# A convolution loop's store moved to another DMA queue, its filter stores made later, and its drain put in another order

## The chip, the cores and the metric

The kernel runs on one core of one Trainium2 chip. That core has TensorE (PE, matrix products[...]), VectorE (DVE), ScalarE (ACT), GpSimd (POOL) and SyncE (SP, which here only starts transfers), and 16 DMA engines. Each engine works through its own instructions in their order; a transfer is started by an instruction of SP, ACT or POOL and runs beside them. The metric is device time of one execution in microseconds, the median of several runs; lower is better.

## The reference

Two blocks in a row, all in float32, batch B = 4, length S = 12544, width D = 128:

```python
h_filt = (np.maximum(pos_emb @ w1, 0) @ w2) * window      # S x D, window = exp(-0.01 * position)
u = x * v
Uf = np.fft.rfft(u, n=2 * S, axis=1)
Hf = np.fft.rfft(h_filt, n=2 * S, axis=0)
y = np.fft.irfft(Uf * Hf, n=2 * S, axis=1)[:, :S]
t = (x * y).reshape(B * S, D)
out = np.maximum(np.maximum(t @ m1, t @ m2), t @ m3) @ m_out   # m1..m3 128 x 768, m_out 768 x 128
```

A long convolution of every channel with one filter, by way of the frequency domain, a gate, and then a feed-forward block with a maximum of three products.

## The kernel before, in words

The transforms are matrix products with tables. A sequence is split in 128 points by 98 blocks; a *first* stage turns each block column into N1 = 90 frequencies (`u_first`, result in `spec`), a *second* stage finishes the forward transform for a pair of frequencies g, the spectrum is multiplied with the filter's, a *third* stage goes back, and its result z is stored in DRAM (`zd`). A last stage, later, reads `zd` (`t_load`), finishes the inverse transform and goes on into the feed-forward block.

The order of all work is written out by hand: every engine gets its instructions in the order in which Python emits them. A prologue (0 to about 117 us) prepares the filter's first stage, the feed-forward weights and the first stage of batch 0. Then comes **the first loop** (lines 992 to 1025, about 117 to 303 us), which the change is about. It runs over s = 0 to 47, with NK = 45 pairs, and is software-pipelined. Iteration s does:

- `s_second(s)` (L943, PSUM `gps`): the filter's second stage on PE, for which POOL has written `minus` (`s_minus`, L931), the negative of a part of its input, one buffer; ACT copies the result to `G` (L948)
- `g_second(s)` (L156, PSUM `ps` in pool `cps`): the data's second stage; ACT copies half of it to `eo` (L187)
- `g_swap(s-1)` on ACT (L547, L548), which makes `xs`
- `s_filter(s-1)` (L961, PSUM `sps`, one buffer of two banks): the filter's spectrum; ACT copies it to `ht` (L966, two buffers), and POOL starts two stores of it to `hd` in DRAM (L969), for the other batches
- `g_third(s-3)` (L156): third stage; ACT copies it to `zs` (L577, two buffers) and ACT itself starts the store to `zd` (L578)
- `g_re`, `g_im`, `g_unfold` of s-2 and `g_butterfly(s)` on DVE (L553, L557, L558, L565, L181, L182): product with the filter (`ht`), unfolding to `ab` for the third stage, and the next input `xt`
- SP starts the loads of the two weight tables, `wf` three iterations ahead for the second stages, and `wi` for the third (L843)

In some of the last iterations there is also work for batch 1: loads (`u_load`), the product x times v on DVE (`u_mul`, L365), and two `u_turn`s at a time, each four transposes on PE (L370) and a copy on ACT (L377).

**The drain** follows: from s = NK on, third stages of the last pairs, six *folds* (`fold`: a transpose of a weight block on PE, L923, a copy `w1t` on ACT, L925, and a product accumulated in `pl`), which give the matrix `lin`, two more turns, and twelve half *units* (`unit`: `u_first` of half a group, PE L417, ACT `high` L426, DVE `spec` L428), the first stage of batch 1. Before, folds and units are strewn between the third stages by the table `drain`.

[...] here three of pool `cps` (tag cv), two of `gps`, two for `sps` and one for `pl`. Before, second and third stages, turns, folds and units all share the three of `cps`.

After the drain, DVE forms `even` from the first loaded `zt` (L678, L679), PE makes the first last-stage products, and the main loop starts with products into `hps` (323.94 us before). From there on PE is busy nearly without a break.

Of the kernel before, what the change touches and what calls it, by code (L numbers as in the profile page):

```python
# [10 lines left out]
FP32 = mybir.dt.float32  # L11
# [5 lines left out]
P = 128  # L17
# [74 lines left out]
def kernel(  # L92
# [15 lines left out]
    nc = tc.nc  # L108
    NG, _, _, B, NB = x.shape
    FO, S = posT.shape  # L110
    D = w2.shape[1]
    DFF = moe_w1.shape[1]
    NF = DFF // P
    NK = N1 // 2
# [7 lines left out]
    hd = dram.tile([NK, P, 512], FP32, name="hd")  # L122
# [29 lines left out]
    def halves_mm(out, lhsT, rhs, start, stop):  # L152


        for h in range(2):
            nc.tensor.matmul(out[64 * h:64 * h + 64], lhsT[:, 64 * h:64 * h + 64], rhs,  # L156
                             start=start, stop=stop, skip_group_check=True)
# [188 lines left out]
    us, uts, ws, hts, eos, xts, xss, abs_, pss, sqs, zss = ({} for _ in range(11))  # L346
# [20 lines left out]
    def turn(u, ps):  # L367
        a, _ = us.pop(u)
        for i in range(4):
            nc.tensor.transpose(ps[0:NB, i * P:(i + 1) * P], a[:, i, :], eye[:])  # L370

    def u_turn(u):
        if u % 2 == 0:
            uts[u] = uts[u + 1] = utp.tile([NB, 16, 2, 32], FP32, tag="uT", name="uT")
        ps = state["turn"].tile([P, 512], FP32, tag="cv", name="pst")
        turn(u, ps)
        nc.scalar.copy(uts[u][:, 8 * (u % 2):8 * (u % 2) + 8],  # L377
                       ps[0:NB, :].rearrange("n (s t r) -> n s r t", s=8, r=2))
# [153 lines left out]
    def g_second(g):  # L532
        ps = state["cv"][1].tile([P, 512], FP32, tag="cv", name="ps2")
        second(ps, ws.pop((g, 0)), g)
        eo = state["cv"][0].tile([P, 2, D], FP32, tag="eo", name="eo", bufs=2)
        evens(ps, eo)
        pss[g], eos[g] = ps, eo

    def g_butterfly(g):
        xt = state["cv"][0].tile([P, 2, 2, D], FP32, tag="x", name="xt", bufs=state["xb"])  # L540
        butterfly(pss.pop(g), eos.pop(g), xt)
        xts[g] = xt
# [8 lines left out]
    def g_re(g):  # L551
        xt = xts[g]
        nc.vector.tensor_tensor(out=xt[:], in0=xt[:], in1=hts[g][:, 0], op=ALU.mult)  # L553

    def g_im(g, apart=False):
        xt, xs = xts[g], xss.pop(g)
        nc.vector.tensor_tensor(out=xs[:], in0=xs[:], in1=hts.pop(g)[:, 1], op=ALU.mult)  # L557
        (nc.gpsimd if apart else nc.vector).tensor_tensor(  # L558
            out=xt[:], in0=xt[:], in1=xs[:], op=ALU.add)

    def g_unfold(g):
        y = xts.pop(g)
        ab = state["cv"][0].tile([P, 2, 2, D], FP32, tag="ab", name="ab", bufs=2)
        for q, op in enumerate((ALU.add, ALU.subtract)):
            nc.vector.tensor_tensor(out=ab[:, :, q, :], in0=y[:, :, 0, :], in1=y[:, :, 1, :],  # L565
                                    op=op)
        abs_[g] = ab

    def g_third(g):
        w, ab = ws.pop((g, 1)), abs_.pop(g)  # L570
        ps = state["cv"][1].tile([P, 512], FP32, tag="cv", name="ps3")
        for k in range(2):
            for q in range(2):
                halves_mm(ps[:, (2 * k + q) * D:(2 * k + q + 1) * D], w[:, k, q, :],
                          ab[:, k, q, :], k == 0 and q == 0, True)
        zs = state["cv"][0].tile([P, 2, 256], FP32, tag="z", name="zs", bufs=2)
        nc.scalar.copy(zs[:].rearrange("p k f -> p (k f)"), ps[:])  # L577
        nc.scalar.dma_start(  # L578
            zd[0][2 * g:2 * g + 2].rearrange("k c t f -> (c t) k f"), zs[:])

    def conv_steps(b, done):
# [259 lines left out]
    def load_dir(g, a):  # L841
        w = lwp.tile([P, 2, 2, P], FP32, tag=f"w{a}", name="wt")
        nc.sync.dma_start(w[:].rearrange("p k r m -> p (k r m)"), wt_d[g, :, a, :])  # L843
        return w
# [31 lines left out]
    for f in range(0, FO, 4):  # L876
        quad([hs[:, f + i] for i in range(4)], (f1h[:, 0], f1h[:, 1]), specH[:, :, :, f:f + 4])
        u, k = divmod(f // 4, 4)
# [27 lines left out]
    for i in (1, 2):  # L906
# [5 lines left out]
    cvp = pro.enter_context(tc.tile_pool(name="cvp0", bufs=3))  # L912
    cps = pro.enter_context(tc.tile_pool(name="cps0", bufs=3, space=PSUM))
    gps = pro.enter_context(tc.tile_pool(name="gps", bufs=2, space=PSUM))
    sps = pro.enter_context(tc.tile_pool(name="sps", bufs=1, space=PSUM))
    state = {"cv": (cvp, cps), "turn": cps, "xb": 2,
             "bank": lambda: cps.tile([P, 512], FP32, tag="cv", name="ps1")}
    pl = sps.tile([D, 512], FP32, name="pl")
    Gs, minus = {}, {}

    def fold(f):
        pt = cps.tile([P, 512], FP32, tag="cv", name="pt")
        nc.tensor.transpose(pt[:, 0:D], w_sb[0][:, f * P:(f + 1) * P], eye[:])  # L923
        w1t = cvp.tile([P, 2, D], FP32, tag="eo", name="w1t", bufs=2)
        nc.scalar.copy(w1t[:, 0], pt[:, 0:D])  # L925
        return lambda: halves_mm(pl[:, 0:D], w1t[:, 0], wo_sb[:, f, :], f == 0, f == NF - 1)

    def s_minus(g):

        m = cvp.tile([P, 2, FO], FP32, tag="minus", name="minus", bufs=1)  # L930
        nc.gpsimd.tensor_single_scalar(m[:], specH[:, 2 * g:2 * g + 2, 0], -1.0, op=ALU.mult)  # L931
        minus[g] = m
# [18 lines left out]
    def s_filter(g):  # L951


        G = Gs.pop(g)
        ps = sps.tile([P, 1024], FP32, tag="h", name="sps")
        for ri in range(2):
            for k in range(2):
                for q in range(2):
                    for h in range(2):
                        at = 512 * q + (2 * ri + k) * D  # L960
                        nc.tensor.matmul(  # L961
                            ps[64 * h:64 * h + 64, at:at + D],
                            G[64 * q:64 * q + 64, k, ri, :], w2x[64 * q:64 * q + 64],
                            start=(ri == 0 and k == 0), stop=True, skip_group_check=True)
        ht = cvp.tile([P, 2, 2, 2, D], FP32, tag="ht", name="ht", bufs=2)
        nc.scalar.copy(ht[:].rearrange("p r k q d -> p (r k) q d"),  # L966
                       ps[:].rearrange("p (q m d) -> p m q d", q=2, d=D))
        for c in range(2):
            nc.gpsimd.dma_start(hd[g, 64 * c:64 * c + 64],  # L969
                                ht[64 * c:64 * c + 64, c].rearrange("p k q d -> p (k q d)"))  # L970
        hts[g] = ht

    EARLY = 6
    loads = dict(zip((NK - 16, NK - 14, NK - 12, NK - 9, NK - 8, NK - 4), range(EARLY)))
    muls = dict(zip((NK - 13, NK - 11, NK - 10, NK - 5, NK - 3, NK - 1), range(EARLY)))
    turns = {NK - 9: 0, NK - 4: 2}
    folded = []

    def folding(f):
        folded.append(fold(f))  # L980
        if len(folded) > 1:
            folded.pop(0)()

    def unit(u):
        for h in range(2):
            u_first(u, 2 * h, 2)

    drain = {NK: [lambda: folding(0), lambda: folding(1), lambda: folded.pop()()],
             NK + 1: [lambda: folding(2), lambda: folding(3), lambda: folded.pop()(),
                      lambda: unit(0), lambda: unit(1)]}  # L990
    s_minus(0)
    for s in range(NK + 3):
        if s < NK:
            ws[s, 0] = wf[s]
            s_second(s)
            if s + 1 < NK:
                s_minus(s + 1)
            g_second(s)
            wf.pop(s)
            if s + 3 < NK:  # L1000
                wf[s + 3] = load_dir(s + 3, 0)
        if 1 <= s <= NK:
            g_swap(s - 1)
            s_filter(s - 1)
        if s >= 3:
            ws[s - 3, 1] = wi.pop(s - 3)
            g_third(s - 3)
            if s < NK:
                wi[s] = load_dir(s, 1)
        if 2 <= s <= NK + 1:  # L1010
            g_re(s - 2)
            g_im(s - 2)
            g_unfold(s - 2)
        if s < NK:
            g_butterfly(s)

        if s in muls:
            u_mul(muls[s])
        if s in turns:
            u_turn(turns[s])  # L1020
            u_turn(turns[s] + 1)
        if s in loads:
            u_load(1, loads[s])
        for job in drain.get(s, ()):
            job()
    u_turn(4)
    u_turn(5)
    folding(4)
    folding(5)
    folded.pop()()  # L1030
    nc.scalar.copy(lin[:], pl[:, 0:D])
    for u in range(2, 6):
        unit(u)
    pro.close()


# [11 lines left out]
    cvp = conv.enter_context(tc.tile_pool(name="cvp", bufs=3))  # L1048
    hps = ctx.enter_context(tc.tile_pool(name="hps", bufs=1, space=PSUM))
    cps = conv.enter_context(tc.tile_pool(name="cps", bufs=1, space=PSUM))  # L1050
# [3 lines left out]
    state = {"bank": lambda: next(pairs)}  # L1054
# [5 lines left out]
    for n, (b, i) in enumerate(tiles[:LAST]):  # L1060
# [7 lines left out]
        for f in range(NF):  # L1068
# [21 lines left out]
            s = i * NF + f  # L1090
# [10 lines left out]
    cps = ctx.enter_context(tc.tile_pool(name="cps2", bufs=1, space=PSUM))  # L1101
    singles = itertools.cycle([cps.tile([P, 512], FP32, name=f"last{i}") for i in range(3)])
    state = {"bank": lambda: next(singles)}
# [86 lines left out]
```

## Time and profile before

Three runs took 2307.21, 2310.24 and 2312.99 us, median 2310.24. The profiled execution spans 2308.4 us at a granted TensorE clock of 0.997.

| Stretch (us) | PE busy | DVE busy | ACT busy | POOL busy | DMA share | GB/s |
|---|---|---|---|---|---|---|
| 150 to 180, first loop | 30.00 | 26.31 | 25.94 | 14.85 | 0.89 | 269 |
| 246 to 257, with loads for batch 1 | 9.95 | 9.18 | 8.33 | 3.90 | 1.02 | 312 |
| 299 to 321, drain | 16.23 | 13.36 | 13.00 | 2.10 | 0.48 | 133 |
| whole, 2308.4 | 2270.3 | 1575.3 | 1179.9 | 899.7 | | |

Busy time of PE is taken from pipelined matmuls whose ends are modelled, so full busy time does not say that PE could go no faster. The instruction that starts a transfer is not counted as busy, although its engine can do nothing else meanwhile: it appears in the order of time as ACTq, POOLq or SPq. Where an engine waited, a line says after which instruction of which engine it went on.

### The profile page before, as it was taken

To read this page: it belongs to the slowest core of one execution; us is meant where nothing else is said; L and a number is where in the kernel's file an instruction comes from. 1 tells how busy PE (TensorE), PEld (TensorE's weight loads), DVE (VectorE), ACT (ScalarE), POOL (GpSimd) and SP (SyncE) were. 2 spreads that over 40 slices of the span, in tenths; PEclk is the share of its full clock that TensorE was granted. 3 is DMA by queue.
4 is the path that set the end of the run, shared out by engine and by line. 5 is a ranking of instruction groups with operands and counts; after the bars stand their busy time and mean duration, and the time that the engine had idled before them with its cause. 6 is when DMAs were issued, how large, how long until landed. Compare 5 with 4: busy or idle time off the path is not lost.

```text
span 2308.4 us, 68374 instructions
## 1 busy us (share of the span) xinstructions
PE 2270.3 (98%) x27855; PEld 1369.0 (59%) x27855; DVE 1575.3 (68%) x2856; ACT 1179.9 (51%) x2128; POOL 899.7 (39%) x1095
## 2 busy tenths in 40 slices
PE   8999989999999999999999999999999999999998
PEld 7989866655555546655555446655555446666665
DVE  5578856767887847758887847658888854445443
ACT  2678844456666534446666624446666632222222
POOL 2045424423333324423333324423333326666666
PEclk9999999999999999999999999999999999999999
DMA  7778969989998759969999849969999932222221
GB/s 176 191 216 266 289 164 190 157 188 241 234 239 221 197 125 192 187 145 240 247 245 247 211 118 194 186 146 244 246 248 240 221 93 55 55 59 68 65 55 22
DMA packets 473164, 411.02 MB, mean 178 GB/s; under 512 B 328005, under 2 KB 374232, under 8 KB 472850
## 3 DMA queue, kind: packets, MB, share of 16 engines
q1 hardware_dynamic: 433714, 317.68, 62.7%
q0 software_dynamic: 26416, 75.80, 11.3%
q10 hardware_dynamic: 12720, 13.18, 1.8%
q8 instruction: 219, 3.59, 0.7%
q14 instruction: 95, 0.78, 0.1%
HBM read 262.84 MB, written 84.67 MB: 151 GB/s over the span
## 4 chain that ended last, share of the span: by engine, by line
PE 83%; DMA 7%; ACT 3%; DVE 3%; issue 2%; SPq 1%; ACTq 0%; POOL 0%; DVEq 0%; POOLq 0%
PE hps L156 40%; PE ops L156 17%; PE ops L773 6%; PE cps L417 5%; PE cps L156 4%; PE ps L165 3%; PE cps L471 3%; PE cps L481 2%; DMA wt<-wq_const 2%; DMA ht<-hd 2%; DMA hd<-ht 2%; PE last L156 1%; ACT ht L966 1%; PE pst L370 1%; DMA zt<-zd 1%
## 5 line engine op out<-in xcount | busy, mean ns | idle before, releaser
L156 PE MATMUL hps<-gt,w_sb 128*64 128x392 f32 x6144 | 1149.6, 495 | 5.8 <-DVE hid L713 5.0
L710 ACT ACTIVATE hid<-hps 128x392 f32<-128x392 f32 x768 | 384.3, 500 | 734.7 <-PE hps L156 718.8
L156 PEld LDWEIGHTS hps<-gt,w_sb 128*64 128x64 f32 x6144 | 422.4, 137 | 438.7 <-issue 390.1
L713 DVE TENSOR_TENSOR hid<-hid,hps 128x392 f32<-128x392 f32 x768 | 427.8, 557 | 334.0 <-PE hps L156 329.6
L156 PE MATMUL ops<-hid,wo_sb 128*64 128x392 f32 x2304 | 477.9, 492 | 0.0
L523 POOL TENSOR_TENSOR cb<-cb,xs 128x512 f32<-128x512 f32 x135 | 181.9, 1347 | 471.7 <-DVE xs L520 327.1
L156 PEld LDWEIGHTS ops<-hid,wo_sb 128*64 128x64 f32 x2304 | 167.7, 137 | 211.5 <-issue 211.5
L496 DVE TENSOR_TENSOR cb<-cps,eo 128x512 f32<-128x512 f32 (+1 forms) x288 | 175.2, 650 | 66.4 <-ACT eo L493 65.9
L428 DVE TENSOR_TENSOR spec<-cps,high 128x360 f32<-128x360 f32 x180 | 135.2, 792 | 122.8 <-ACT high L426 122.8
L728 POOL DMA_DIRECT2D out_dram<-ot x96 | 75.1, 783 | 353.5 <-ACT ot L726 311.5
L511 ACT ACTIVATE xs<-cb 32x512 f32<-32x512 f32 x270 | 170.0, 630 | 22.6 <-DVE cb L496 13.9
L512 ACT COPY xs<-cb 32x512 f32<-32x512 f32 x270 | 166.7, 617 | 3.2
L426 ACT COPY high<-cps 128x360 f32<-128x360 f32 x90 | 71.9, 799 | 152.4 <-PE cps L417 125.7
L527 DVE TENSOR_TENSOR xs<-cb 128x256 f32<-128x256 f32 x270 | 142.0, 569 | 7.5 <-POOL cb L523 7.5
L417 PEld LDWEIGHTS cps<-f1q,uT 98*64 98x64 f32 x2880 | 124.1, 137 | 31.3 <-issue 30.6
L417 PE MATMUL cps<-f1q,uT 98*64 98x90 f32 x2880 | 127.7, 241 | 0.4 <-DVE uT L401 0.4
L386 POOL COPY planes<-ut 128x784 uint16<-128x784 uint16 x90 | 75.8, 842 | 113.0 <-DVE ut L365 110.2
L504 POOL DMA_DIRECT2D zd<-cb x135 | 92.9, 690 | 61.5 <-DVE cb L496 53.5
L156 PEld LDWEIGHTS cps<-f4p,even 90*64 90x64 f32 x1568 | 88.8, 138 | 37.6 <-issue 34.8
L515 DVE TENSOR_TENSOR cb<-cb,ht 128x512 f32<-128x512 f32 x135 | 92.3, 683 | 7.8 <-ACT xs L512 7.7
L156 PE MATMUL cps<-f4p,even 90*64 90x49 f32 x1568 | 95.7, 220 | 1.8 <-DVE even L678 1.8
L156 PE MATMUL cps<-f4p,zt 90*64 90x49 f32 x1568 | 97.0, 222 | 0.4 <-DVE zt L679 0.4
(137 smaller groups left out, 3195.7 us busy)
## 6 DMA issues: line engine op xcount, KB each, us to landing
ht<-hd SPq DMA_DIRECT2D x264, 256.0 KB, 6.8
wt<-wq_const SPq DMA_DIRECT2D x144, 256.0 KB, 6.8
zd<-cb POOLq DMA_DIRECT2D x135, 256.0 KB, 6.2
zt<-zd SPq DMA_DIRECT2D x384, 90.0 KB, 3.1
sq<-spec SPq DMA_DIRECT2D x264, 128.0 KB, 7.2
ut<-in_xr_dram SPq DMA_DIRECT2D x128, 196.0 KB, 4.3
ut<-in_vr_dram SPq DMA_DIRECT2D x128, 196.0 KB, 4.5
xT<-in_x_dram SPq DMA_DIRECT2D x256, 98.0 KB, 3.5
```

Of the source, the lines that this page charges most:

```text
L156: nc.tensor.matmul(out[64 * h:64 * h + 64], lhsT[:, 64 * h:64 * h + 64], rhs, start=start, stop=stop, skip_group_check=True)
L417: nc.tensor.matmul(ps[64 * c:64 * c + 64, 256 * i + h * N1:256 * i + (h + 1) * N1], t[:, 2 * ((at + i) % 8) + h].rearrange("n r t -> n (r ...
L428: nc.vector.tensor_tensor(out=spec[:, :, a, at:at + n], in0=v[:, 1], in1=high, op=op)
L496: nc.vector.tensor_tensor(out=cb[:, a, lo:hi], in0=ps[:, lo:hi], in1=eo[:, lo:hi], op=op)
L504: nc.gpsimd.dma_start(zd[b][2 * z:2 * z + 2].rearrange("k c t a f -> (k c t) a f"), zss.pop(z))
L511: nc.scalar.mul(xs[at:at + 32], xt[at + 32:at + 64], -1.0)
L512: nc.scalar.copy(xs[at + 32:at + 64], xt[at:at + 32])
L523: nc.gpsimd.tensor_tensor(out=xts[g], in0=xts[g], in1=xs[:], op=ALU.add)
L527: nc.vector.tensor_tensor(out=ab[:, q], in0=y[:, 0], in1=y[:, 1], op=(ALU.subtract, ALU.add)[q])
L710: nc.scalar.activation(h[:], pa[:, 0:N], Relu)
L713: nc.vector.tensor_tensor(out=h[:], in0=h[:], in1=pb[:, 0:N], op=ALU.max)
L773: nc.tensor.matmul(ps[64 * c:64 * c + 64, 0:H2], w, rhs[:, H2 * c:H2 * c + H2], start=start, stop=True, skip_group_check=True)
```

## The change

It has four parts, all in the first loop and its drain. First, the store of z is started by SP and not by ACT, so that ACT is spared the trigger. Second, the two stores of the filter's spectrum leave `s_filter` and become `s_store(g)`, emitted one iteration later, so that on POOL the next `minus` no longer stands behind a store that waits for ACT. Third, the turns inside the loop get a PSUM bank of their own (the one that later holds `pl`), and are made one an iteration in four iterations, not two in two. Fourth, in the drain both last products with the filter (`re`, `im`, `unfold` of 43 and 44) are emitted at s = NK, only unit 0 stands among the third stages, and folds, turns and the other units follow after them in turn; units, folds' turns and `w1t` get other buffers: units rotate over the two banks of `gps` and the three of `cps`, and `w1t` takes the buffers of `G`.

```diff
@@ u_turn
-        ps = state["turn"].tile([P, 512], FP32, tag="cv", name="pst")
+        ps = state["turn"]()
@@ g_third
-        nc.scalar.dma_start(
+        nc.sync.dma_start(
             zd[0][2 * g:2 * g + 2].rearrange("k c t f -> (c t) k f"), zs[:])
@@ pools
-    state = {"cv": (cvp, cps), "turn": cps, "xb": 2,
-             "bank": lambda: cps.tile([P, 512], FP32, tag="cv", name="ps1")}
-    pl = sps.tile([D, 512], FP32, name="pl")
+    free = itertools.cycle([(gps, "g"), (cps, "cv")])
+    def bank():
+        pool, tag = next(free)
+        return pool.tile([P, 512], FP32, tag=tag, name="ps1")
+    state = {"cv": (cvp, cps), "xb": 2, "bank": bank,
+             "turn": lambda: sps.tile([P, 512], FP32, tag="pl", name="pst")}
@@ fold
-        w1t = cvp.tile([P, 2, D], FP32, tag="eo", name="w1t", bufs=2)
+        w1t = cvp.tile([P, 2, D], FP32, tag="G", name="w1t", bufs=2)
@@ s_filter, s_store
-        for c in range(2):
-            nc.gpsimd.dma_start(hd[g, 64 * c:64 * c + 64],
-                                ht[64 * c:64 * c + 64, c].rearrange("p k q d -> p (k q d)"))
         hts[g] = ht
+    def s_store(g):
+        for c in range(2):
+            nc.gpsimd.dma_start(
+                hd[g, 64 * c:64 * c + 64],
+                hts[g][64 * c:64 * c + 64, c].rearrange("p k q d -> p (k q d)"))
@@ loop
-    turns = {NK - 9: 0, NK - 4: 2}
+    turns = {NK - 9: 0, NK - 8: 1, NK - 4: 2, NK - 3: 3}
-    drain = {NK: [lambda: folding(0), lambda: folding(1), lambda: folded.pop()()],
-             NK + 1: [lambda: folding(2), lambda: folding(3), lambda: folded.pop()(),
-                      lambda: unit(0), lambda: unit(1)]}
...
-        if 2 <= s <= NK + 1:
-            g_re(s - 2)
-            g_im(s - 2)
-            g_unfold(s - 2)
+        for g in {NK: (s - 2, s - 1)}.get(s, (s - 2,)):
+            if 0 <= g < NK and s <= NK:
+                s_store(g)
+                g_re(g)
+                g_im(g)
+                g_unfold(g)
...
             u_turn(turns[s])
-            u_turn(turns[s] + 1)
...
-        for job in drain.get(s, ()):
-            job()
-    u_turn(4)
-    u_turn(5)
-    folding(4)
-    folding(5)
+        if s == NK:
+            unit(0)
+    pl = sps.tile([P, 512], FP32, tag="pl", name="pl")
+    state["turn"] = bank
+    for f, then in enumerate(((unit, 1), (unit, 2), (u_turn, 4), (u_turn, 5), (unit, 3), None)):
+        folding(f)
+        if then:
+            then[0](then[1])
     folded.pop()()
     nc.scalar.copy(lin[:], pl[:, 0:D])
-    for u in range(2, 6):
-        unit(u)
+    unit(4)
+    unit(5)
```

More of the change, by code (lines that the diff above doesn't have):

```diff
@@ L967, in s_filter @@
                        ps[:].rearrange("p (q m d) -> p m q d", q=2, d=D))
+        hts[g] = ht
+    def s_store(g):
         for c in range(2):
-            nc.gpsimd.dma_start(hd[g, 64 * c:64 * c + 64],
-                                ht[64 * c:64 * c + 64, c].rearrange("p k q d -> p (k q d)"))
-        hts[g] = ht
+            nc.gpsimd.dma_start(
+                hd[g, 64 * c:64 * c + 64],
+                hts[g][64 * c:64 * c + 64, c].rearrange("p k q d -> p (k q d)"))
     EARLY = 6
```

## The prediction

> **What bounds the kernel now.** The whole page says PE 98% busy, but the change touches only the first loop and its drain, so I read that stretch alone, starting with busy time by stretch (stretch, its length, then busy us of PE, its weight loads, DVE, ACT, POOL, the clock, the DMA share and GB/s):
>
> ```profile
> 150.00:180.00 30.00, 30.00 (x604) 27.44 (x600) 26.31 (x55) 25.94 (x46) 14.85 (x22) 1.00 0.89 269
> 299.00:321.00 22.00, 16.23 (x310) 13.90 (x310) 13.36 (x37) 13.00 (x29) 2.10 (x4) 1.00 0.48 133
> ```
>
> In the loop PE, DVE and ACT all look nearly full; in the drain none does. So the loop asks which engine is really back to back, and the drain which waits end last. Next, ACT in order of time, one iteration (start, duration, engine, line):
>
> ```profile
> 270.10 0.59 ACT L577 COPY zs<-ps 128x512 f32<-128x512 f32 x1
> 270.73 0.37 ACTq L578 DMA_DIRECT2D zd<-zs  x1
> 271.13 0.37 ACT L948 COPY G<-gps 128x256 f32<-128x256 f32 x1 [0.44 <-ACT zs L577]
> 271.40 0.38 ACT L187 COPY eo<-ps 128x256 f32<-128x256 f32 x1
> 271.81 0.63 ACT L547 ACTIVATE xs<-xt 64x512 f32<-64x512 f32 x1
> 272.45 0.62 ACT L548 COPY xs<-xt 64x512 f32<-64x512 f32 x1
> 273.09 1.02 ACT L966 COPY ht<-sps 128x1024 f32<-128x1024 f32 x1
> ```
>
> ht starts at 269.19 and at 273.09, 3.90 apart (3.90 to 3.95 in undisturbed iterations, 3.94 typical), with no gap but the 0.44 before G, which is the trigger of z's store (the ACTq line). **ACT is the bound**, and the trigger is part of it. How far below lies PE? The chain shows an iteration where PE led:
>
> ```profile
> 131.56 0.87 PE gps L943 x16
> 132.44 0.87 PE ps L156 x16
> 133.31 1.03 PE sps L961 x32
> 134.34 1.02 PE ps L156 x16
> 135.37 0.87 PE gps L943 x16
> ```
>
> 135.37 - 131.56 = 3.81 us. PE also runs 269.35, 273.16, 276.96, 280.77 after a turn: 3.81 each. DVE, from unfold to unfold with no wait (178.28 to 181.98), takes 3.70. So ACT's lead over PE is only 0.13 us an iteration. The waits from 140 to 262 us and the page of line 969 give the second bound:
>
> ```profile
> POOL hd L969 <- ACT ht L966: 58.8, 31, 3.3
> ACT ht L966 <- DMA hd<-ht: 2.8, 6, 1.6
> ...
> DMA to landing us min/median/max: 2.3/4.7/7.5
> ```
>
> POOL sits in front of the filter's store until ht is copied, and six times ACT waits for the older store to land before it may overwrite ht. POOL's wait is harmless except at the start:
>
> ```profile
> 125.35 0.45 POOL hd L969
> 125.96 0.57 POOL hd L969
> 126.55 0.95 POOL minus L931
> 127.54 0.98 PE gps L943 x13
> ```
>
> There minus is queued behind a store, and PE idles 0.90 for it. Last, the drain, by its waits from 262 to 321 us and the SP queue:
>
> ```profile
> PEld pl L156 <- ACT w1t L925: 3.9, 3, 2.2
> PE pst L370 <- DVE xt L182: 1.9, 2, 1.1
> ...
> 313.89 1.88 SPq L654 DMA_DIRECT2D zt<-zd  x2
> ```
>
> PE stands 3.3 us for the folds' copies. Both in-loop turns wait for the butterfly (1.9). The first zt load goes out 2.3 us after the last z trigger (311.62): that store's landing.
>
> [...] z's store now shares SP's row with the weight loads (256 KB each). This trace has no such store; I bound it below. [...] minus takes 0.54 at its shortest and 1.01 in the median[...]
>
> **The change, part by part.**
>
> 1. *Minus ahead of the store* (s_store after s_minus). Removes the 0.90 and its neighbour waits at the start: **-1.0 us**. Later minus has slack (PE waited 0.8 in 41 iterations).
>
> 2. *Trigger from ACT to SP.* ACT falls from 3.90 to 3.90 - 0.44 = 3.46; the bound becomes PE's 3.81. From gps at 131.56 to the last filter product (299.26) are 167.7 us and 41 iterations. At PE's pace: 41 x 3.81 = 156.2, plus four turns' transposes at 0.58 (0.62 and 0.61 in the chain, less overlap) = 2.3, sum 158.5. **Headroom 9.2 us**; it holds 5.3 of trigger (41 x 0.13), about 1.0 of the turn iterations (before they cost 5.58 and 5.60, two times 1.66 over normal, 3.3 against 2.3: the spare turn bank ends the wait for the butterfly) and the 2.8 of store waits. On SP the store waits for zs; behind it stands the load of wi[s], which needs the same third stage finished anyhow and has three iterations (11.4 us) for a landing of 4.4. So SP costs nothing, unless z's store lands late: zs has two buffers, so it may take about 2 x 3.8 - 0.59 - 0.7 = 6.3 us; landing on ACT's row was 5.0 median, 7.1 most.
>
> 3. *The filter's store an iteration later.* With PE leading, put gps(k+2) at 0. Its reads of minus end near 0.95; minus(k+3) takes up to 1.0; the store's first trigger 0.57 ends at 2.55. ht(k), by ACT's order, ends at 0.65, so the store leaves 1 us later than it could. Landing L later, ht(k+2) is copied (1.0 with its latencies 1.2) and must be done when the filter product after next starts, at 2 x 3.81 + 1.9. Allowed: L = 9.5 - 2.55 - 1.2 = 5.75. Before, ht to ht with 2 x 3.94 less 1.87 to the end of the trigger and 0.1 allowed 5.9. Nearly the same tolerance, so I expect nearly the same waits, a little more frequent: of 44 pairs about 10 landed at 5.8 to 7.5, with an excess over 5.75 of 4.6 in sum; about three quarters of it delays PE: **+3.5 us given back** (bounds: 0 if bursts get shorter, 7 if latency grows by half a microsecond). The bytes per iteration do not change (1.02 MB, 269 GB/s at 3.94, 278 at 3.81; 312 were carried from 246 to 257).
>
> 4. *Drain.* Set the last filter product at 0 (299.26); before, the last unit's product ended at 319.61, +20.35. After: third(42) to 2.1, unit 0 to 3.4, third(43) to 4.6. DVE does re, im, unfold of 43 from 0.67 (after ht(43)) and of 44 behind it, 2.9 each, to 6.5: PE waits 1.9 for it, third(44) to 7.6. Left for PE: five units at 1.24 (48 products in 1.86 us, 38.8 ns, 32 a unit), six folds at 0.22 + 0.33, two turns at 0.58: 6.2 + 3.3 + 1.2 = 10.7, so 18.3; 0.5 for copies that arrive late: 18.8. **-1.5 us** (bounds 0 and -3). ACT has 8.3 us of work in the same stretch (ten copies high at 0.49, six w1t at 0.22, two uT at 0.59, zs 0.59, lin 0.27) and DVE 6.6 (22 times 0.30), so neither passes PE if the five banks take up the latency. zt: zs(44) to 8.3, trigger and landing 2.6, two issues 1.9, landing 3.8: 16.6, hidden behind the units, whose DVE pair ends 1.3 after PE. After that the main loop follows as before; it is PE back to back, so the shift is kept.
>
> Sum: -1.0 - 9.2 + 3.5 - 1.5 = **-8.2 us**; 2310.24 - 8.2 = 2302.0.
>
> **Rivals.**
>
> *The stores bind.* For: DMA share 0.89, and SP's loads and z's store now start within one microsecond of the filter's stores. If L is 5.9 in the mean, an iteration is (5.9 + 1.87)/2 = 3.89: loop 41 x 3.89 + 2.3 = 161.8, gain 5.9; less 1.7 for the u loads' bursts (the longest wait of before was 1.6), plus 1.0 at the start, the drain's gain lost to a DVE backlog (two u products of 0.56 in the last three iterations): -5.2, **2305.0**. Against: the bytes of an iteration are the same and were absorbed at a median of 4.7. Chance 0.25.
>
> *Clean.* The waits vanish, since ACT with 0.35 spare catches up: -11.7, **2298.5**. For: every direct wait was on the bounding engine. Chance 0.12.
>
> *Slower.* One shared row stretches landing: at L = 6.8 (the 245 to 253 stretch had 5.7 to 7.5 with two more loads) an iteration is 4.33, loop 179.8, +12.1, less 2.5: **2320**. For: the store leaves 1 us later and only two ht buffers. Against: total traffic is the same and is drained within an iteration. Chance 0.08.
>
> **How the numbers follow.** Forecast 2302.0 with 0.55. The 0.3% limit is 6.9 us, 2303.3; the forecast's own spread passes it in four of five (0.44), clean always (0.12), the stores' case seldom (0.03): faster 0.59. Slower 0.08, the rest 0.33. Range 2297.5, below clean, to 2308, which holds the stores' case with the drain's gain at zero; only slower lies outside, with the tails.
>
> **What would show it.** Right: the ACTq gap before G gone, ht to ht near 3.83, PE gps to gps at 3.81, 4.4 in turn iterations; no POOL wait on ht ahead of minus; the first zt load near 303 to 304 us (now 313.89); the first hps product about 8 us ahead of 323.94. Step 3 is wrong if ACT's wait for the filter's store is far from 3 to 4 us, or if zs waits for z's store. Step 4 is wrong if PE still idles for w1t or ends its units later than +19.5. The prediction as a whole falls if the landing median of the filter's store rises above 5.3.

## The result, and the profile after

| | Before | After |
|---|---|---|
| time, median of 6 runs each (us) | 2309.92 | 2300.94 |
| lowest and highest | 2307.21, 2312.99 | 2298.29, 2304.76 |
| profiled span | 2308.4 | 2299.5 |

The ratio is 0.9962, with a 95% interval of 0.9949 to 0.9976: faster by 9.0 us, where 8.2 was forecast (2302.0). The sum was nearly right; its terms were not all. To see where the 8.9 us between the two profiles came from, I cut both at the same instructions of PE: the first product into `gps`, the third filter product (into `sps`), the last filter product, the end of the last unit, and the first `hps` product.

| Stretch on PE (us) | Before | After | Difference | Forecast |
|---|---|---|---|---|
| up to the first `gps` product | 117.79 | 116.88 | -0.91 | 0 |
| start, to the third filter product | 11.65 | 10.32 | -1.33 | -1.0 |
| loop, third to 45th filter product | 169.82 | 162.80 | -7.02 | -5.7 |
| drain, from there to the end of the last unit | 20.35 | 20.41 | +0.06 | -1.5 |
| tail, to the first `hps` product | 4.33 | 5.16 | +0.83 | 0 |
| all the rest | 1984.46 | 1983.93 | -0.53 | 0 |

The first row is not the change's: before, the granted clock was 0.50 from 36.5 to 39.9 us, and after it was 1.00 there. Two readings stand out: the loop gave more than forecast, and the drain gave nothing.

**The loop.** ACT of the changed kernel in order of time, one iteration (the columns are those shown of before):

```profile
202.75 0.59 ACT L577 COPY zs<-ps 128x512 f32<-128x512 f32 x1
203.23 0.39 ACT L953 COPY G<-gps 128x256 f32<-128x256 f32 x1
203.97 0.37 ACT L187 COPY eo<-ps 128x256 f32<-128x256 f32 x1 [0.35 <-PE ps L156]
204.37 0.63 ACT L547 ACTIVATE xs<-xt 64x512 f32<-64x512 f32 x1
205.01 0.62 ACT L548 COPY xs<-xt 64x512 f32<-64x512 f32 x1
205.65 1.01 ACT L971 COPY ht<-sps 128x1024 f32<-128x1024 f32 x1
```

The ACTq line and the 0.44 before `G` are gone, so that `G` starts 0.48 after `zs` and not 1.03, and a new gap of 0.35 stands before `eo`, which ends on PE. That is the sign of a bound that has moved: ACT now waits once an iteration for PE. The chain of waits is accordingly PE after PE, 205.93 - 202.12 = 3.81:

```profile
202.12 0.87 PE gps L948 x16
203.00 0.87 PE ps L156 x16
203.87 1.03 PE sps L966 x32
204.91 1.02 PE ps L156 x16
205.93 0.87 PE gps L948 x16
```

The filter's store did bite, but seldom. The chain at its longest stall, and then the waits from 140 to 262 us, the stretch of the prediction (waiting instruction, what it waits for, total, times, longest):

```profile
168.73 0.53 POOL hd L977
169.26 6.74 DMA hd<-ht
...
176.10 1.02 ACT ht L971
...
177.17 1.10 PE sps L966 x32
```

```profile
ACT ht L971 <- DMA hd<-ht: 5.5, 8, 1.4
...
POOL hd L977 <- ACT ht L971: 2.3, 4, 1.1
```

A store that took 6.74 to land kept ACT from overwriting `ht`, and PE's next filter product came 4.31 after the one before. But of the 5.5 us that ACT waited, PE lost little: over the loop, filter products stood more than 3.81 apart in only three iterations without a turn (4.31, 4.02, 4.07), 1.0 us over the normal in all. In the chain the first two hang on a store's landing, and the third on no store that the trace names. ACT's spare hid the rest. POOL's wait in front of the store fell from 58.8 in 31 to 2.3 in 4.

**The drain.** PE in order of time:

```profile
296.59 1.17 PE L156 MATMUL ps<-ab,wt 128*64 128x128 f32 x16 [2.09 <-DVE ab L565]
297.69 0.33 PE L928 MATMUL pt<-eye,w_sb 128*128 128x128 f32 x1
297.95 2.29 PE L417 MATMUL ps<-f1q,uT 98*64 98x90 f32 x32
...
305.39 1.41 PE L417 MATMUL ps<-f1q,uT 98*64 98x90 f32 x32
```

The unit after the 2.09 wait takes 2.29, the later one 1.41, for the same 32 products of the same shape. Busy time by stretch gives the reason; the columns are stretch and length, then busy us (and instructions) of PE, PEld, DVE, ACT, POOL, then the granted clock, DMA share and GB/s:

```profile
293.00:297.00 4.00, 1.88 (x32) 1.43 (x30) 3.12 (x8) 2.52 (x5) 1.04 (x2) 1.00 0.72 195
298.50:301.50 3.00, 3.00 (x35) 2.57 (x33) 1.20 (x4) 1.25 (x4) 0.00 (x0) 0.50 0.43 131
302.00:310.00 8.00, 7.95 (x144) 6.57 (x142) 3.21 (x11) 5.00 (x14) 0.87 (x1) 1.00 0.54 144
312.50:318.50 6.00, 5.02 (x42) 3.17 (x44) 1.09 (x2) 0.50 (x1) 0.00 (x0) 0.50 0.26 70
```

The clock falls to 0.50 in the drain at 298.39, 1.8 us after the end of the gap of 2.09, and again where the main loop begins, at 312.05, when PE had stood idle for 1.64. In the records of the first loop, the drain and the tail such a fall lasts 3.41 us or a multiple of it (298.39 to 301.81, and 312.05 to 318.87, here), and each such piece costs, where PE has work all the time, half of that, 1.71 us. In the drain of before there was none. So the drain lost 1.7 us to the clock, and the tail, within the second fall, 0.8.

The 2.09 is not all work of DVE. ACT waited for a store to land before it could copy the last `ht`, and DVE for that copy:

```profile
292.89 1.01 ACT L971 COPY ht<-sps 128x1024 f32<-128x1024 f32 x1 [1.18 <-DMA hd<-ht]
```

```profile
293.94 0.69 DVE L553 TENSOR_TENSOR xt<-xt,ht 128x512 f32<-128x512 f32 x1 [0.75 <-ACT ht L971]
```

### The profile page after: what moved, and what is told of

It reads as the page before. It is cut to its first block, busy times and chain, and to the rows that moved or that the text cites. A ratio compares the mean times of both kernels' runs of the same rounds, so it can differ in the third digit from the quotient of the medians.

```text
span 2299.5 us, 68542 instructions
## 1 busy us (share of the span) xinstructions
PE 2266.3 (99%) x27855; PEld 1371.0 (60%) x27855; DVE 1573.0 (68%) x2856; ACT 1175.9 (51%) x2128; POOL 883.0 (38%) x1095
## 4 chain that ended last, share of the span: by engine, by line
PE 89%; DMA 5%; DVE 2%; issue 1%; SPq 1%; ACT 1%; POOL 0%; DVEq 0%; POOLq 0%; ACTq 0%
PE hps L156 40%; PE ops L156 17%; PE ops L773 6%; PE cps L417 5%; PE cps L156 4%; PE ps L156 3%; PE ps L165 3%; PE cps L471 3%; PE cps L481 2%; DMA ht<-hd 2%; PE sps L966 2%; PE gps L948 2%; PE last L156 1%; DMA zt<-zd 1%; DMA wt<-wq_const 1%
```

## The experiments

Two theories stood at the outset for the pieces. One: the loop's gain is the trigger's, capped by PE's 3.81, and the drain lost its gain to the clock. Its rival: the later store, or a backlog in DVE and ACT, is what spoiled the drain and gave back part of the loop. The ratios are to the kernel before, each from five rounds of both kernels on one chip.

### One part at a time

The trigger alone, on the kernel before:

```diff
-        nc.scalar.dma_start(
+        nc.sync.dma_start(
             zd[0][2 * g:2 * g + 2].rearrange("k c t f -> (c t) k f"), zs[:])
```

> The kernel before with only the store of z started by SP. Theory T1 (the trigger on ACT is what bounds the loop): an iteration falls from 3.94 to about 3.81 us, 5 to 7 us off the total; the start still loses its 1.3 us and the turn iterations stay near 5.4. Rival T2 (POOL's wait of 86.6 us in front of the filter's store is what holds the loop, the trigger only rides along): iteration stays at 3.9, total within 1 us of before.

2306.29 us, ratio 0.997 (0.9959 to 0.9981). In the chain of waits the filter products follow at 3.81:

```profile
225.27 1.03 PE sps L961 x32
...
229.08 1.03 PE sps L961 x32
```

So moving the trigger by itself makes PE the bound. POOL's wait in front of the filter's store stayed (57.9 in 32 from 140 to 262 us, 58.8 in 31 before), so it is not what held the loop. ACT's wait for the store to land was 2.3 in 4. The surprise is in the drain, which was left as it was and still fell from 20.35 to 18.78.

The later store alone, on the kernel before:

```diff
-        for c in range(2):
-            nc.gpsimd.dma_start(hd[g, 64 * c:64 * c + 64], ...)
...
+            s_store(s - 2)
             g_re(s - 2)
```

> The kernel before with only the filter's store emitted an iteration later. T1: 1.3 us off at the start of the loop, the iteration stays at 3.94, total 1 us less than before. T2: iteration near 3.81 and 5 us or more off the total.

2309.46 us, ratio 0.9988 (0.9982 to 0.9995). The start shortens by 1.32, as in the full change; ACT is still back to back with its trigger:

```profile
203.19 0.37 ACTq L578 DMA_DIRECT2D zd<-zs  x1
203.59 0.37 ACT L948 COPY G<-gps 128x256 f32<-128x256 f32 x1 [0.44 <-ACT zs L577]
```

`ht` starts 3.88 apart there (201.66, 205.54), 3.89 typical, against 3.94 before. The difference lies right behind the trigger (from its start to that of `G` 0.41 in the median, 0.45 before); what makes it is not explained.

The drain, the turns and their banks alone, that is the changed kernel with both stores put back:

```diff
-        nc.sync.dma_start(
+        nc.scalar.dma_start(
             zd[0][2 * g:2 * g + 2].rearrange("k c t f -> (c t) k f"), zs[:])
...
-                s_store(g)
                 g_re(g)
```

> Only turns, banks and drain of the change; z's store on ACT, the filter's store early. T1: turn iterations win about 1 us, the drain nothing, because PE's 2 us of idleness ahead of the last third stage lets its clock drop to half: total 0 to 2 us under before. If the new drain itself is good and only the stores' landing spoils it in the changed kernel: 2.5 us or more under before and no drop of the clock between third stages and units.

2308.16 us, ratio 0.9985 (0.9975 to 0.9994), 3.8 us under before. Of the two expectations the second came true. The drain takes 18.11, DVE goes from pair 43 to pair 44 without a wait for `ht`, and the unit after the gap is not slow:

```profile
302.90 1.17 PE L156 MATMUL ps<-ab,wt 128*64 128x128 f32 x16 [1.61 <-ACT zs L577]
...
304.25 1.46 PE L417 MATMUL ps<-f1q,uT 98*64 98x90 f32 x32
```

And both store moves, with turns, banks and drain as before (shown against the changed kernel):

```diff
-        ps = state["turn"]()
+        ps = state["turn"].tile([P, 512], FP32, tag="cv", name="pst")
...
-    turns = {NK - 9: 0, NK - 8: 1, NK - 4: 2, NK - 3: 3}
+    turns = {NK - 9: 0, NK - 4: 2}
...
+    drain = {NK: [lambda: folding(0), ...], NK + 1: [...]}
```

> Both moves of stores, but turns, banks and drain of the kernel before. T1: loop start and iteration as in the changed kernel, turn iterations with the wait for the butterfly still there (about 1 us more in all), drain about as long as the changed one's (20.4 us from the last filter product to the last unit) since the changed drain won nothing: total 6.5 to 8.5 us under before. If the new drain is worth the 1.5 us that were predicted: 5 to 6.5 us under before.

2305.55 us, ratio 0.9965 (0.9954 to 0.9977). By whole times that can't be told from the full change; by PE's landmarks it can. Its loop is 165.97, 3.2 us longer: 2.9 of it because its two turn iterations take 7.20 and 6.18 against four of 4.53, the rest in longer stalls elsewhere. The second turn waits for the butterfly, which lost its place on the only three banks:

```profile
260.07 0.61 PE L370 MATMUL pst<-eye,ut 128*98 128x128 f32 x4 [2.05 <-DVE xt L182]
```

In one table, all relative to before (us; the drain also with the time lost to the half clock taken off, 1.71 for each piece seen in its trace):

| Kernel | start | loop | drain | drain without half clock |
|---|---|---|---|---|
| trigger alone | 0.0 | -4.9 | -1.6 | -1.6 |
| later store alone | -1.3 | -1.9 | +1.3 | -0.4 |
| drain and turns alone | 0.0 | -1.5 | -2.2 | -2.2 |
| sum of the three | -1.3 | -8.2 | -2.5 | -4.2 |
| both stores, old drain | -1.3 | -3.9 | +0.3 | -1.4 |
| all (the change) | -1.3 | -7.0 | +0.1 | -1.6 |

The start belongs to the later store, the loop to the trigger and, for 2.9 us of it, to the turns. The column of the loop is to be read with care: five traces whose loop is the changed one up to the stores of its last pairs took from 162.1 to 164.1 us for it, so that 1 us there can be stores that landed late and not the part. In the drain, trigger (18.78) and new order (18.11) remove largely the same waits: with both it would be 18.7 at full clock. Once the trigger is off ACT, the new order of the drain is worth little: the old order took 18.8 and 18.9, the new one, in the changed kernel and three variants below, 18.2 to 18.7, all without the lost pieces and one trace each.

### How much ACT has to spare

These two give ACT added work whose result nothing uses: one or three copies of 128 by 128 an iteration, into `lin`, which is overwritten later.

```diff
         nc.scalar.copy(zs[:].rearrange("p k f -> p (k f)"), ps[:])
+        for _ in range(1):
+            nc.scalar.copy(lin[:], w2x[:])
         nc.sync.dma_start(
```

> The changed kernel with one extra copy of 128 x 128 on ACT (about 0.25 us of it) behind each copy zs, where the trigger of z's store was. If PE's 3.81 us are the bound of the loop now and ACT has 0.35 to spare, nothing moves: iteration 3.81, total within 1 us of the changed kernel. If ACT still bounds the loop: 0.25 an iteration, 10 us or more longer.

2302.01 us, ratio 0.9962 (0.995 to 0.9974): the iteration stays at 3.805 and the loop is 162.52. The copy takes 0.20 us of ACT (the next one starts so much later than it), and this costs nothing, so ACT is not the bound.

With `range(3)`:

> The changed kernel with three such copies an iteration (about 0.7 us). ACT then needs about 4.15 us and bounds the loop again: iteration 4.1 to 4.2, 11 to 16 us longer than the changed kernel and longer than the kernel before. If ACT's work is hidden altogether: no difference.

2317.45 us, ratio 1.0023 (1.0016 to 1.003). PE's filter products, each now waiting for ACT's `ht`:

```profile
229.42 1.10 PE L968 MATMUL sps<-w2x,G 64*64 64x128 f32 x32 [0.54 <-ACT ht L973]
...
233.63 1.10 PE L968 MATMUL sps<-w2x,G 64*64 64x128 f32 x32 [0.33 <-ACT ht L973]
```

They are 4.21 apart. ACT in the same iteration:

```profile
229.74 0.97 ACT L579 COPY lin<-w2x 128x128 f32<-128x128 f32 x3
230.62 0.37 ACT L955 COPY G<-gps 128x256 f32<-128x256 f32 x1
```

The three copies take 0.88 from start to start. So ACT's own pace without them is 3.33, and at PE's 3.81 it has 0.48 to spare. The prediction had 3.46 and 0.35, since it took the price of the trigger from the idle gap of 0.44. But ACT's copies overlap: after the change `G` starts 0.48 after `zs`, although `zs` lasts 0.59, and before it started 1.03 after it. The trigger took 0.55 of ACT's order.

### What costs the drain its gain

Busy work for PE in the gap of 2.09, products that nothing uses (18 calls of the half products with `eye`, ahead of the last third stage). They lasted 4.1 us, twice what was planned, so they also held the last third stage up, by 1.4:

```diff
+            if s == NK + 1:
+                keep = state["turn"]()
+                for _ in range(18):
+                    halves_mm(keep[:, 0:P], eye[:], eye[:], True, True)
```

> The changed kernel with 36 products of eye with eye (about 2 us of PE, result unused) between the last two third stages, where PE stands idle for 2.1 us. If the clock's drop to half is what costs the drain its gain: no drop, unit 1 takes 1.3 us and not 2.2, the last unit ends about 18.5 to 19 us after the last filter product and not 20.4, total 1 to 2 us less than the changed kernel. If the units wait for ACT or for banks: the same 20.4.

2307.41 us, ratio 0.9982 (0.9975 to 0.9988), slower than the changed kernel by its ratio; but the clock stays full in the drain, and the first unit after the gap takes 1.46, not 2.29:

```profile
293.76 4.10 PE L156 MATMUL pst<-eye 128*64 128x128 f32 x72
297.69 1.04 PE L156 MATMUL ps<-ab,wt 128*64 128x128 f32 x16
298.92 1.46 PE L417 MATMUL ps<-f1q,uT 98*64 98x90 f32 x32
```

The drain was 20.15: 1.7 won on the clock, 1.4 lost to the filler. The tail grew to 6.20: PE waited 1.30 for DVE's `zt`, which by my reading then ran beside POOL's sums for the next tile. This agrees with the clock as the cause. It does not yet exclude the later store as the cause of the gap itself.

So next the stores of the last pairs went back to their old place in `s_filter`, the rest staying later:

```diff
         hts[g] = ht
+        if g >= NK - 3:
+            s_store(g)
...
-                s_store(g)
+                if g < NK - 3:
+                    s_store(g)
                 g_re(g)
```

> The changed kernel, but the filter's stores of the last three pairs leave at once, as in the kernel before (no minus is left for them to block). If the late store is what spoils the drain: ACT's wait of 1.18 us before the last copies ht goes, PE's gap before the last third stage shrinks from 2.1 to about 1.6, no drop of the clock in the drain, last unit near 18.1 after the last filter product as in the kernel with the drain alone, 2 us less than the changed kernel in total. If the gap is only the VectorE work of two pairs: unchanged 20.4.

2304.84 us, ratio 0.9969 (0.9958 to 0.9981). It missed its aim by its order: store 41, still late, now came after store 42 on POOL, and `ht` of 43 needs the buffer of 41. POOL waited 3.29 for `ht` of 42 with store 41 behind it, ACT then 4.70 for the landing, and PE longer still:

```profile
297.20 1.98 PE L966 MATMUL sps<-w2x,G 64*64 64x128 f32 x32 [5.46 <-ACT ht L971]
```

With store 41 ahead of 42:

```diff
+        if g == NK - 3:
+            s_store(g - 1)
+        if g >= NK - 3:
+            s_store(g)
...
+                if g < NK - 4:
+                    s_store(g)
```

> As the kernel with the last stores early, but in their right order: the store of pair 41 ahead of that of pair 42. If the late store is what spoils the drain: the 5.5 us stall of that kernel is gone, no wait of ACT for a landing before the last copies ht (1.18 in the changed kernel), the gap ahead of the last third stage falls from 2.1 to 1.6 or less, last unit 18.1 us after the last filter product and not 20.4, total 2 us less than the changed kernel. If VectorE's two pairs alone make the gap: 2.1 and 20.4 again.

2304.04 us, ratio 0.9963 (0.9953 to 0.9974). ACT's wait for a store before the last `ht` is shorter, but not gone, and PE's gap stays:

```profile
296.20 1.01 ACT L971 COPY ht<-sps 128x1024 f32<-128x1024 f32 x1 [0.87 <-DMA hd<-ht]
```

```profile
299.89 1.17 PE L156 MATMUL ps<-ab,wt 128*64 128x128 f32 x16 [2.04 <-DVE ab L565]
...
301.25 1.46 PE L417 MATMUL ps<-f1q,uT 98*64 98x90 f32 x32
```

The store now leaves as soon as its `ht` is copied, so what holds the last `ht` is its landing and no longer its lateness. DVE waits 0.45 for that `ht` (0.75 in the changed kernel), and the last third stage starts 6.29 after the last filter product and not 6.59. So the lateness delays that stage by about 0.3 us. Of the gap of 2.04, DVE's two pairs make about 1.6, which is also the gap of the drain alone, where nothing waits for a landing; DVE's wait makes the rest. And this time the clock stayed at 1.00 after a gap of 2.04, and the drain took 18.56. A gap of about 2 us can cost a drop of the clock and need not.

Last, the changed kernel with only the filter's store back in its old place:

```diff
+        for c in range(2):
+            nc.gpsimd.dma_start(hd[g, 64 * c:64 * c + 64],
...
-    def s_store(g):
...
-                s_store(g)
                 g_re(g)
```

> The changed kernel with the filter's store back at its old place, ahead of the next minus. If the later store earns only the start and costs the drain: start 1.3 us slower (11.65 from the first gps to the third filter product), iteration 3.81, last unit 18.1 after the last filter product and not 20.4: total within 1.5 us of the changed kernel. If the later store is needed for the loop: iteration above 3.85 and total 3 us or more longer.

2304.88 us, ratio 0.997 (0.9959 to 0.9981). The start is 11.63 again, the loop 163.41. The drain is the longest of all, 23.34, with no late store in it:

```profile
299.35 1.17 PE L156 MATMUL ps<-ab,wt 128*64 128x128 f32 x16 [2.14 <-DVE ab L565]
...
300.85 2.67 PE L417 MATMUL ps<-f1q,uT 98*64 98x90 f32 x32
```

```profile
300.50:310.00 9.50, 9.50 (x87) 7.40 (x86) 2.49 (x9) 3.69 (x10) 0.00 (x0) 0.50 0.51 133
```

Three pieces at half clock, 5.1 us lost; without them 18.2. The rival, that the lateness of the store spoils the drain, falls with this run and the last stores in order: without it the gap is as long and the clock falls or does not. What stays of it is that DVE waits 0.45 to 0.75 us of the gap for `ht` in the changed kernel and in these two, behind a store's landing where the trace names the cause, late or not.

### Can both be had

The run with the last stores in order, and eight calls of half products (32 recorded, 1.92 us, result unused) between the last unit and the first last-stage product, to keep PE busy where the clock falls a second time:

```diff
             t_sums(tiles[0], nc.vector)
+            keep = ops.tile([D, 512], FP32, tag="ops", name="ops")
+            for _ in range(8):
+                halves_mm(keep[:, 0:P], w_sb[1][:, 0:P], w_sb[1][:, 0:P], True, True)
             t_last(tiles[0])
```

> As last_stores_in_order, and PE does 8 unused products (1.7 us) between the last unit and the first last-stage product, where it stands idle for 1.9. If that idleness halves the clock at the start of the main loop (3.4 us of it in the kernel before, 6.8 in the changed one): no drop there, the first hps product 4.3 us after the last unit falls to about 4.2 and the following 3.4 to 6.8 us run at full clock, 1.7 to 3.4 us less in total. If the clock falls for another reason: the drop stays and the total does not move.

2302.6 us, ratio 0.9964 (0.995 to 0.9979). The main loop now begins at full clock:

```profile
315.00:321.00 6.00, 5.80 (x36) 3.17 (x38) 1.74 (x4) 1.49 (x3) 0.00 (x0) 1.00 0.67 145
```

Its profile is the shortest of all (2296.7), but its time can't be told from the changed kernel's. Part is lost again: in the tail DVE and POOL now work at the same time,

```profile
311.72 1.64 DVE L679 TENSOR_TENSOR zt<-zt 90x512 f32<-90x512 f32 x1
```

which takes 0.69 where POOL is idle. And its drain, with a gap of 2.09, lost one piece of 3.41 us at half clock again.

The last run adds to it useful work in the gap: unit 1 and two folds ahead of the last third stage, on the banks of `gps` and of the filter product.

```diff
+        if s == NK + 1:
+            two = sps.tile([P, 1024], FP32, tag="h", name="two")
+            wide += [two[:, 0:512], two[:, 512:1024]]
+            folding(0)
+            unit(1)
+            folding(1)
```

> As in_order_kept_busy, and unit 1 and two folds are moved into PE's gap ahead of the last third stage, on the two banks that the filter products no longer need. If PE's order bounds the drain: the gap shrinks by up to 1.6, last unit 16.5 to 17 us after the last filter product, 1 to 1.5 us less than in_order_kept_busy. If ACT and VectorE bound it: 18 as there, no gain.

2302.91 us, ratio 0.9962 (0.995 to 0.9973). The gap moved and grew:

```profile
299.16 1.47 PE L417 MATMUL two<-f1q,uT 98*64 98x90 f32 x16 [3.17 <-DVE spec L428]
```

The drain took 22.27, two pieces at half clock in it. In this order PE can't be fed there: the unit's copies come behind `re`, `im` and `unfold` on DVE. None of these kernels is faster than the changed one beyond its interval.

## Why the prediction was nearly right, step by step

**Step 1, minus ahead of the store: right.** -1.0 forecast, -1.33 measured, and the later store alone gives -1.32. At the start of the changed kernel POOL's order is minus, then the store:

```profile
123.41 0.53 POOL L936 TENSOR_SCALAR minus<-specH 128x128 f32<-128x128 f32 x1 [2.41 <-PE gps L948]
124.42 1.17 POOL L977 DMA_DIRECT2D hd<-ht  x2 [0.48 <-ACT G L953]
```

**Step 2, the trigger: right in mechanism, its headroom too large.** "ACT is the bound" and "the bound becomes PE's 3.81" are shown by the trigger alone and by the two runs with ACT copies. The loop checks: 41 iterations of 3.805, the last of 2.91 (it has no second stages), four turns at 0.725 over the normal and 1.0 of stalls make 156.0 + 2.9 + 2.9 + 1.0 = 162.8, as measured. But the headroom of 9.2 was 1.3 too large. It put 41 iterations between a `gps` product and the last filter product; from that `gps` product to its own filter product there is 1.75 more, the last iteration is 0.9 shorter, and 3.805 for 3.81 takes off 0.2, which leaves 0.65 more. And the turns were put at 0.58 each and take 0.725, 0.6 more for the four. ACT's 3.46 was wrong too (3.33, above), which cost nothing, since PE is the bound.

Of the terms within the headroom, the gain of the turns was put at 1.0. Between filter products before's two turn iterations took 6.21 and 5.99, 4.6 over 3.805; after, four take 2.9: a gain of 1.7. With PE as the bound it is larger still, 2.9 against the run with the old drain. z's store on SP cost nothing in the loop, as forecast: `zs` waited for it once, in the drain. From 140 to 262 us the queue of the weight loads moved 26.1 MB and not 17.3, with z's store in it; the store landed in 4.6 (5.0 before) and the weight loads in 5.4 (4.5 before), which nothing waited for.

**Step 3, given back to the store: over-sized.** "I expect nearly the same waits ... about three quarters of it delays PE: +3.5 us given back." ACT waited 5.5 in 8 up to 262 us, more than the 3 to 4 that I named, but PE's stalls in the loop were 1.0 in sum. The term that failed is the three quarters. ACT's spare of 0.48 an iteration and the two buffers hide most of a late landing; of the 5.5, PE saw a fifth at most. A later wait of 1.2, in the drain, is part of the gap there. The prediction set ACT's order as fixed to PE's and let nearly all pass. The rival in which the stores bind (2305.0) needed a mean landing of 5.9: the median is 4.7, as it was. The slower rival needed 6.8.

**Step 4, the drain: wrong.** "18.3; 0.5 for copies that arrive late: 18.8. -1.5 us." Its working held in number up to the gap: the last third stage ended at 7.76 (7.6 forecast), after a wait of 2.09 (1.9), though up to 0.75 of that wait was the landing of a store, which the working did not have. At full clock the units would have ended at +18.7, against 18.8. But the clock fell for one piece of 3.41 us in the drain, and again at the tail, so that 20.41 and +0.83 were measured. That is beyond the +19.5 that was named as the sign of being wrong. The first `zt` load did go out early, at 300.80 (303 to 304 forecast), but DVE sums `zt` only behind the last unit. The wait was priced by its own length, and what an idle PE costs afterwards was left out. And the step booked as the drain's what the trigger earns too: with the old drain and the trigger moved, it ends at 18.78.

The errors offset: loop 1.3 better than forecast (2.5 less given back to the store, 1.3 too much headroom), start 0.3, prologue 0.9 and rest 0.5 by no doing of the change, drain and tail 2.4 worse. That the sum came within 1 us is in good part luck.

**Left open.** A gap of 2.0 to 2.1 us was followed by no half clock (last stores in order), by one piece (the change, and the run kept busy), by two (one copy on ACT) or by three (store not later). What decides between them was not shown. The traces show when the clock changed: the half clock begins at 19.45, 36.51 and 323.23 us in the kernel before, and at 18.50, 298.39 and 312.05 us in the changed kernel, and within each of the two traces these times lie a whole number of 3.413 us apart (5 and 89, and 82 and 86, after the first). Two kernels with the same drain up to the last unit can be set side by side with stretches of that length. In each pair of lines the first is the stretch in which the gap begins, the second the next one, with borders reckoned from the falls in the same trace; the columns are those of the stretches above. Last stores in order, then the same kept busy:

```profile
296.17:299.58 3.41, 1.68 (x38) 1.44 (x33) 2.82 (x6) 2.63 (x5) 1.05 (x2) 1.00 0.79 212
299.58:302.99 3.41, 3.10 (x52) 2.52 (x54) 1.86 (x8) 1.39 (x4) 0.00 (x0) 1.00 0.63 189
```

```profile
292.90:296.31 3.41, 1.32 (x26) 1.11 (x22) 2.71 (x7) 2.17 (x5) 1.04 (x2) 1.00 0.72 202
296.31:299.73 3.42, 3.42 (x37) 2.77 (x36) 1.06 (x5) 0.75 (x2) 0.00 (x0) 0.50 0.59 158
```

In the first, a border cut the gap in two, 1.73 and 0.31 us idle, and the clock stayed at 1.00; in the second the gap lay whole in one stretch, 2.09 us idle, and the clock was 0.50 in the next. That the place of the gap made the difference is my reading of this pair and was not shown. The idle time in a stretch does not decide it alone: ahead of the fall in the changed kernel's drain it was 1.61, less than the 1.73 that no fall followed. Only one profile of each kernel was taken, so whether the same kernel falls differently from run to run isn't shown either. Why a fall lasts one, two or three pieces stays open, as do the 0.05 us of the later store alone, and the spread of the time after the first `hps` product between kernels that don't differ there (1981.5 to 1988.1 us).

## What to carry to other kernels

Find the engine that runs back to back, and count the instructions that start its transfers, which no busy time shows; take one away, and the gain ends where the next engine's pace begins (here 0.13 us of the 0.55 that the trigger took). Price it from start to start, since an idle gap between copies that overlap shows less (0.44). Two parts that relieve the same engine don't add: price each with the others in place. An idle gap of about 2 us on PE can cost as much again after it, when the clock falls (1.71 after the 2.09 of the changed kernel), and its length alone did not decide whether it fell (after 2.04 and 2.09, in two kernels with the same drain, it fell once, for 3.41 us); so put work into such a gap only if it does not hold up what ends the gap.

## What the runs showed of the hardware that was not expected

- The half clock (0.50 granted) came in pieces of 3.41 us, 1.71 us lost in each that PE could have filled, after PE gaps of 2.09 us (the change) and 2.14 (store not later), among others; a gap of 2.04 (last stores in order) and one of 1.61 (the drain alone) brought none.
- A transfer's trigger on ScalarE took 0.55 us of its order (`zs` to `G` 1.03 with it, 0.48 without), where the trace shows 0.37 for the instruction and 0.44 of idle time.
- VectorE's sum `zt` of 90 by 512 took 0.69 alone (last stores in order) and 1.64 while GpSimd made the sums of the same size for the next tile (1.51 and 1.60 long, in the run kept busy).
